# The sum over keys as one instruction, the residual through PSUM, and low halves on GpSimd or VectorE: a four-layer attention and MLP kernel

## The chip, the cores and the metric

The kernel runs on one core of a Trainium2 chip. The core has TensorE (PE, matmuls into the accumulator memory PSUM; its weight loads are PEld), VectorE (DVE), ScalarE (ACT), GpSimd (POOL) and the queue engine SyncE (SP), which issues nearly all DMAs here. Each engine works through its own instructions in order and waits on semaphores of the others. The metric is the device time of one execution in microseconds (us), the median of several runs. A profile is taken in a run of its own.

## What is computed

x has 2048 rows of 640. Four layers follow each other, two of attention (the same weights both times) and two of an MLP:

```python
x = x + _A_ref(_layernorm(x), A_wqkv, A_wo)     # 32 heads of 20; each row looks at 8 keys,
x = x + _B_ref(_layernorm(x), B_w1, B_b1, ...)  # at distance 0, 2, 4, ... 14 behind it
x = x + _A_ref(_layernorm(x), A_wqkv, A_wo)     # MLP: layernorm, 640 -> 1536, gelu, 1536 -> 640
x = x + _B_ref(_layernorm(x), B_w1, B_b1, ...)
...
logits = jnp.einsum("bhsd,bhswd->bhsw", q, kg) * scale
attn = _softmax(logits, axis=-1)
o = jnp.einsum("bhsw,bhswd->bhsd", attn, vg)
```

## The kernel before, in words

**Units.** The distance of two between keys splits the rows into even and odd ones, and each parity into two halves: four units of 512 rows. A unit lies on 128 partitions with four rows each (M = 4, index t). With two attention layers there are eight units of attention, n = 0 to 7; n // 4 is the layer. Each unit has four groups of eight heads, 32 groups in all, G = 4 n + g.

**Precision.** A matmul on 16-bit operands takes every 32-bit operand as a high half and a low half (low = value - high), and adds three products: high x high, high x low, low x high (PASS). So every tensor that goes into a matmul needs an instruction for its high half (ScalarE) and one for its low half. The low halves that matter here: `yl`, of the layer-normed rows (line 617, 640 wide, VectorE); `ol`, of the attention output (line 779, 640 wide, GpSimd for the first three groups of a unit and VectorE for the fourth); `hlo`, of the MLP's hidden values (line 859, 512 wide, or 256 wide for the first unit, VectorE). Weights are kept times 64 (WS).

**One unit.** `layernorm` makes y and its halves and has the DMA transpose them. `qkv` multiplies (line 647), ScalarE copies the result (line 664), and it goes out to DRAM (`spill`), from which `fetch` brings q, k and v back, each partition with the rows of its neighbours that its windows need. `attention(G)` does the rest on VectorE, for two of the four rows at a time (a = 0, 1): multiply q with eight windows of k (line 731, 2560 elements), sum over the 20 elements of a head (line 735, a reduce from 2560 to 128), the softmax on 256 elements (lines 740 to 750, with the exponential on ScalarE; lines 743 and 748 reduce over the eight keys, which lie apart in memory), multiply with eight windows of v (line 757, 2560), and sum over the eight keys by halves: 1280, 640 and 320 elements (lines 765 and 769). `project(n)` transposes the output by DMA, multiplies it with wo in eight products of 15 matmuls (line 803, two column halves of 320 for each t), and line 809 on VectorE adds the result to x. Then `layernorm(..., True)` and `mlp`: line 848 multiplies into a PSUM bank, ScalarE applies gelu (line 854) and takes the high half (line 857), VectorE the low half (line 859), and line 869 multiplies into accumulators. Line 624 on GpSimd adds the bias b2 to x ahead of that. The last two units' MLP is done jointly by `joint` and `pair` with fewer products (lines 907 to 1233); its weights are loaded (line 961) into the buffers `pr`, once the last attention is done with them.

**Order.** Nothing is scheduled by the compiler. Every instruction is entered in a `Plan` with its engine, an estimated duration, a priority, what it needs and gives, and the buffers it uses. `Plan.run` then simulates the core: at each step it takes the engine that can start first and, on it, the ready instruction with the lowest priority number; the order found in this way is the order of the instructions on every engine and queue. Durations are formulas: `v_cost(n)` = 0.067 + n/960 us for VectorE (line 282), plus 0.19 for the reduces of lines 743 and 748, and `a_cost` for ScalarE (line 286). The chip follows the order; it does not follow the times.

**GpSimd beside VectorE.** The plan marks VectorE instructions that read two tensors from SBUF (`PAIRS`, line 66, by the name of what they give) and GpSimd instructions that do so (`pair=True`). For a marked GpSimd instruction the plan looks for a time outside the stretches of marked VectorE instructions (lines 197 to 203), and a marked VectorE instruction is planned after a marked GpSimd instruction that runs longer than 1 us (line 192). Such a GpSimd instruction also gets a dependency on the VectorE instruction planned to end before it (`behind`, lines 269 and 1285). `ol` on GpSimd waits besides for the first multiply of the next group (line 782), and line 624 for certain later groups (line 623), so that both fall beside the reduce of line 735; they are booked at ASIDE = 1.7 us.

**Buffers that matter.** `ps`: three PSUM banks, shared by qkv, the projection and the MLP's first product; `w`: five, for y, its halves and the attention output; `pr`: two, for the products of attention; `h32` and `hh`: two and three, for the hidden values.

Of the kernel before, what the change touches and what calls it, by code (L numbers as in the profile page):

```python
# [12 lines left out]
OP = mybir.AluOpType  # L13
# [52 lines left out]
PAIRS = ("qk", "pv", "ad", "o", "sub", "at", "hlo", "yl", "xb", "ol", "wq", "lo", "lm")  # L66

TURN = 2.7

# [4 lines left out]
class Plan:  # L74
# [35 lines left out]
    def add(self, eng, dur, prio, emit, need=(), give=(), use=(), table=None, move=None, lazy=False, wait=None,  # L110
            pair=False):
        o = dict(eng=eng, dur=dur, prio=prio, emit=emit, need=need, give=give, use=use, table=table,
                 move=move, lazy=lazy, n=len(self.ops), pair=pair,
                 wait=self.PATIENCE * (eng == "dve" and prio < -200) if wait is None else wait)
        self.ops.append(o)
        for u in use:
            if u not in self.users and u[0] in self.ORDERED and u not in self.line.setdefault(u[0], []):
                self.line[u[0]].append(u)
            self.users[u] = self.users.get(u, 0) + 1

    def run(self):
# [3 lines left out]
        left = {}  # L125
        for o in self.ops:
            left[o["n"]] = len(set(o["need"]))
            for k in set(o["need"]):
                waiting.setdefault(k, []).append(o)
            if not left[o["n"]]:  # L130
                ready.setdefault(o["eng"], []).append(o)
# [10 lines left out]
        def done(o, end, lag):  # L142
            for u in o["use"]:
                self.users[u] -= 1
                self.last[u] = max(self.last.get(u, 0.0), end + lag * (u[0] != "pr" or o["eng"] != "dve"))
                if not self.users[u]:
                    self.free[u[0]].append((self.last[u], self.slot[u]))
            for k in o["give"]:
                when[k] = (o["eng"], end, bool(o["move"]))
                for w in waiting.pop(k, ()):  # L150
                    left[w["n"]] -= 1
                    if not left[w["n"]]:
                        ready.setdefault(w["eng"], []).append(w)
# [32 lines left out]
        def start(o):  # L186
            t = clock[o["eng"]]
# [3 lines left out]
            if o["pair"] and o["eng"] == "dve":  # L191
                t = max(t, port)
            for k in o["need"]:
                e, w, moved = when[k]
                w = w + (self.LAG["sp"] + self.SPARE[o["eng"]] if moved else self.LAG[e] if e != o["eng"] else 0.06 * (e != "pe"))
                t = max(t, w)
            if o["pair"] and o["eng"] == "pool":
                for i, (a, b) in enumerate(reversed(shut)):
                    if t >= b:
                        break  # L200
                    if a <= t:
                        t = b + 0.1 * (i == 0)
                        break
            new = {}
            for u in o["use"]:
                if u in self.slot:
                    t = max(t, self.since[u])
                else:
                    fs = self.free[u[0]]
                    if u[0] in self.ORDERED and self.line[u[0]][self.turn.get(u[0], 0)] != u:  # L210
                        return None
                    i = new.get(u[0], 0)
                    if i >= len(fs):
                        return None
                    t = max(t, sorted(fs)[i][0])
                    new[u[0]] = i + 1
            return t

        total = len(self.ops)
        while len(order) < total:  # L220
            best = None
            for e, ops in ready.items():
                pick = None
                for o in ops:
                    t = start(o)
# [5 lines left out]
                if pick and (best is None or (pick[1], pick[0]) < (best[1], best[0])):  # L231
                    best = pick
            then = event()
            if best is None and then == math.inf:
# [4 lines left out]
            _, t, o = best  # L239
            e = o["eng"]  # L240
            ready[e].remove(o)
            d = o["dur"]
# [24 lines left out]
            elif e == "pool" and o["pair"] and d > 1:  # L267
# [22 lines left out]
def sliding_dilated_then_mlp_kernel(  # L290
# [128 lines left out]
    def pool(dur, prio, emit, need=(), give=(), use=(), pair=False):  # L419
        plan.add("pool", dur, prio, emit, need, give, use, pair=pair)  # L420
# [120 lines left out]
    def layernorm(n, prio, yk, twice):  # L541
# [56 lines left out]
        for t in range(m):  # L598
# [13 lines left out]
            if n == 0 and not twice:  # L612
# [4 lines left out]
            dve(D, first(t), lambda key=key, parts=parts: nc.vector.tensor_sub(parts()[:, 1], tile_of(*key), parts()[:, 0]),  # L617
                need=[("yh", name, t)], give=[("yl", name, t)], use=[key, nk, hk])
# [3 lines left out]
            if twice and n != PAIR[0]:  # L622
                G, a = NG * n + ((6, 1), (7, 1), (8, 0), (8, 1))[t][0], (1, 1, 0, 1)[t]
                pool(ASIDE, -200 + n, lambda t=t: nc.gpsimd.tensor_add(x[u][:, t], x[u][:, t], b2),  # L624
                     need=[("y", name, t), ("qk", G, a), "b2"], give=[("xb", n, t)], pair=True)
# [73 lines left out]
    def attention(G):  # L699
# [52 lines left out]
        for a in range(NE):  # L752
# [10 lines left out]
            last = ("pv", G, a)  # L763
            for w in (4, 2):
                dve(EH * w * GC, G - 0.9, lambda vk=vk, w=w: nc.vector.tensor_add(  # L765
                    tile_of(*vk)[:, :, 0:w], tile_of(*vk)[:, :, 0:w], tile_of(*vk)[:, :, w:2 * w]),
                    need=[last], give=[("ad", G, a, w)], use=[vk])
                last = ("ad", G, a, w)
            dve(EH * GC, G - 0.9, lambda vk=vk, t0=t0: nc.vector.tensor_add(
                ot()[:, t0:t0 + EH], tile_of(*vk)[:, :, 0], tile_of(*vk)[:, :, 1]),  # L770
                need=[last], give=[("o", G, a)], use=[vk, ok])
# [9 lines left out]
        if g < NG - 1:  # L781
            pool(ASIDE, -300 + G, lambda: lo(nc.gpsimd), need=[("oh", G), ("qk", G + 1, 0)], give=[("ol", G)], use=[ok, hk],
                 pair=True)
        else:
            dve(m * GC, -300 + G, lambda: lo(nc.vector), need=[("oh", G)], give=[("ol", G)], use=[ok, hk])

    def project(n):
# [3 lines left out]
        for t in range(m):  # L791
            dma_transpose(-600 + n, lambda t=t: nc.sync.dma_start_transpose(
                transposed(yk)[:, :, t * P:(t + 1) * P], tile_of(*hk)[:, t].rearrange("p a b -> p (a b)")),
                need=[("ol", n * NG + g) for g in range(NG)], give=[("oT", n, t)], use=[hk, yk])
        for t in range(m):
            for c in range(2):
                pk = ("ps", ("wo", n, t, c))

                def product(t=t, c=c, pk=pk):
                    i = 0  # L800
                    for k in range(KD):
                        for a, b in PASS:
                            nc.tensor.matmul(tile_of(*pk)[:, :D // 2], transposed(yk)[:, a * KD + k, t * P:(t + 1) * P],  # L803
                                             wo[:, b, k, c * D // 2:(c + 1) * D // 2], start=i == 0, stop=i == 3 * KD - 1)
                            i += 1

                def residual(t=t, c=c, pk=pk):
                    xs = x[u][:, t, c * D // 2:(c + 1) * D // 2]
                    nc.vector.scalar_tensor_tensor(xs, tile_of(*pk)[:, :D // 2], 1.0 / WS, xs, op0=OP.mult, op1=OP.add)  # L809

                mm(3 * KD * D // 2, 15, -600 + n, product, need=[("oT", n, t), *[("lo", ("o", k)) for k in range(KD)]],
                   give=[("wop", n, t, c)], use=[pk, yk])
                dve(D // 2, -700 + n, residual, need=[("wop", n, t, c)], give=[("xh", n, t, c)], use=[pk])
# [4 lines left out]
    def mlp(at, b, t0, t1):  # L818
# [17 lines left out]
        for e in range(NF):  # L836
# [7 lines left out]
            def inner(ck=ck, pk=pk):  # L844
# [14 lines left out]
            dve(nt, -1000, lambda h32=h32, hk=hk: nc.vector.tensor_sub(  # L859
                tile_of(*hk)[:, 1, :nt], tile_of(*h32)[:, :nt], tile_of(*hk)[:, 0, :nt]),  # L860
                need=[("hhi", j)], give=[("hlo", j)], use=[h32, hk])
# [454 lines left out]
```

## Time and profile before

| | us |
|---|---|
| median of 3 runs | 1147.57 |
| lowest, highest | 1146.56, 1148.22 |
| the profiled execution | 1150.09 |
| its span, first to last instruction | 1148.3 |

The page of the profile gives busy times of each engine, the chain of work that ended last, and groups of instructions. A group's row reads: line, engine, operation, output<-input with shapes, xcount | busy us, mean ns of one | idle time of the engine ahead of it and what ended it. In the timeline the columns are start, duration, engine, line, operation. L12 is line 12 of the kernel before. In the view of waits a row is: engine and line <- what ended its wait: total us, times, longest.

### The profile page before, as it was taken

The numbers are of one execution on the slowest core, as the hardware profiler recorded it, in microseconds if no ns is written. First come the engines' busy times: TensorE is split into PE (matmuls) and PEld (weight loads), VectorE is DVE, ScalarE is ACT, GpSimd is POOL, SyncE is SP. The second block draws the span as 40 slices with busy tenths as digits, with TensorE's granted clock in tenths as the row PEclk, the third lists the DMA queues.
The fourth block names the chain that finished last, engine by engine and source line by source line (L and its number), as shares of the span: only waits on it lengthen the run. The fifth ranks groups of instructions, "written<-read, shape, count | busy, mean of one in ns | idle before, by whom it ended". The sixth has DMA issues, their size and how long they took to land.

```text
span 1148.3 us, 17448 instructions
## 1 busy us (share of the span) xinstructions
PE 1138.7 (99%) x6834; PEld 629.9 (55%) x6834; DVE 1070.0 (93%) x1099; ACT 551.5 (48%) x989; POOL 111.9 (10%) x94
## 2 busy tenths in 40 slices
PE   9999999999999999999999999999999999999998
PEld 6444446577664455545555554556456555644476
DVE  7899999999999999999999999999999998599982
ACT  6385435536355336732637362375333533477630
POOL 1010001011012102210112011101110000000000
PEclk9999999999999999999999999999999999999999
DMA  9999999888875587577475956567756754796201
GB/s 302 297 305 266 299 342 280 279 265 258 242 202 188 171 230 165 184 201 220 131 225 159 216 157 211 180 180 176 214 181 174 200 194 134 192 249 180 62 25 69
DMA packets 239791, 235.47 MB, mean 205 GB/s; under 512 B 139020, under 2 KB 195164, under 8 KB 239708
## 3 DMA queue, kind: packets, MB, share of 16 engines
q1 hardware_dynamic: 239708, 234.36, 69.6%
q8 instruction: 53, 0.87, 0.3%
q14 instruction: 30, 0.25, 0.1%
HBM read 157.55 MB, written 44.78 MB: 176 GB/s over the span
## 4 chain that ended last, share of the span: by engine, by line
PE 91%; DVE 4%; DMA 2%; issue 1%; ACT 1%; SPq 0%; POOL 0%; POOLq 0%; ACTq 0%
PE ps L647 34%; PE acc L869 19%; PE ps L848 18%; PE ps L803 11%; PE acc L1041 3%; PE ps L1076 3%; PE ps L1041 2%; DVE pr L973 1%; DVE pr L731 1%; PE acc L1237 1%; DMA c<-mw 1%; DMA yT<-ohl 1%; PE acc L1076 1%; DVE yT L988 0%; DMA yT<-w 0%
## 5 line engine op out<-in xcount | busy, mean ns | idle before, releaser
L647 PE MATMUL ps<-wq,yT 128*128 128x480 f16 (+1 forms) x1950 | 391.2, 363 | 0.5 <-DMA yT<-w 0.3
L647 PEld LDWEIGHTS <-yT 128*128 128x128 f16 x1950 | 189.2, 98 | 199.3 <-DMA yT<-w 0.7
L869 PE MATMUL acc<-c,act 128*128 128x512 f16 (+1 forms) x1728 | 248.3, 299 | 0.1
L848 PE MATMUL ps<-yT,c 128*128 128x512 f16 (+1 forms) x1260 | 246.5, 349 | 1.0 <-DMA c<-mw 1.0
L869 PEld LDWEIGHTS <-act 128*128 128x128 f16 x1728 | 136.0, 98 | 106.1 <-issue 0.4
L731 DVE TENSOR_TENSOR pr<-qk 128x2560 f32<-128x2560 f32 x64 | 180.6, 2823 | 4.6 <-DMA qk<-spill 4.4
L735 DVE TENSOR_REDUCE sm<-pr 128x128 f32<-128x2560 f32 x64 | 179.7, 2810 | 0.1
L757 DVE TENSOR_TENSOR pr<-sm,v 128x2560 f32<-128x2560 f32 x64 | 179.5, 2820 | 0.3
L848 PEld LDWEIGHTS <-c 128*128 128x128 f16 x1260 | 120.2, 98 | 107.8 <-DMA c<-mw 1.7
L664 ACT ACTIVATE ev<-ps 128x480 f32<-128x480 f32 x128 | 72.5, 567 | 181.1 <-PE ps L647 167.9
L765 DVE TENSOR_TENSOR pr<-pr 128x1280 f32<-128x1280 f32 (+1 forms) x128 | 144.8, 1153 | 0.1
L803 PE MATMUL ps<-wo,yT 128*128 128x320 f16 x960 | 131.9, 299 | 0.7 <-DMA yT<-ohl 0.7
L854 ACT ACTIVATE act<-ps,b 128x512 f32<-128x512 f32 (+1 forms) x84 | 52.4, 624 | 164.8 <-PE ps L848 164.4
L803 PEld LDWEIGHTS <-yT 128*128 128x128 f16 x960 | 93.8, 98 | 38.7 <-DMA yT<-ohl 1.1
L569 ACT ACTIVATE junk<-xf 128x640 f16<-128x640 f32 x57 | 41.9, 735 | 80.4 <-DVE xf L809 68.3
L779 POOL TENSOR_TENSOR ohl<-w,ohl 128x640 f16<-128x640 f32 x24 | 34.2, 1427 | 365.1 <-DVE pr L731 215.5
L586 POOL TENSOR_TENSOR ln<-ln,half 128x2 f32<-128x2 f32 (+1 forms) x31 | 34.9, 1126 | 340.8 <-ACT ln L583 340.6
L859 DVE TENSOR_TENSOR act<-act 128x512 f16<-128x512 f32 (+1 forms) x84 | 51.2, 610 | 9.5 <-ACT act L857 9.2
L624 POOL TENSOR_TENSOR xf<-xf,b 128x640 f32<-128x640 f32 x24 | 37.9, 1578 | 165.2 <-DVE act L859 61.9
L609 ACT ACTIVATE w<-xf,ln 128x640 f32<-128x640 f32 x53 | 47.1, 909 | 3.1 <-DVE w L617 3.1
L857 ACT ACTIVATE act<-act 128x512 f16<-128x512 f32 (+1 forms) x84 | 47.5, 566 | 2.0
L573 ACT ACTIVATE junk<-xf,ln 128x640 f16<-128x640 f32 x57 | 46.9, 822 | 0.8
(194 smaller groups left out, 955.9 us busy)
## 6 DMA issues: line engine op xcount, KB each, us to landing
c<-mw SPq DMA_DIRECT2D x174, 320.0 KB, 3.7
spill<-ev SPq DMA_DIRECT2D x64, 480.0 KB, 4.2
qk<-spill SPq DMA_DIRECT2D x32, 880.0 KB, 5.8
v<-spill SPq DMA_DIRECT2D x32, 880.0 KB, 5.3
qk<-spill SPq DMA_DIRECT2D x32, 320.0 KB, 3.2
act<-in_B_w_dram SPq DMA_DIRECT2D x24, 320.0 KB, 4.9
mw<-c SPq DMA_DIRECT2D x24, 320.0 KB, 4.9
pr<-in_B_w_dram SPq DMA_DIRECT2D x24, 320.0 KB, 3.8
```

Source lines behind the costliest of these rows:

```text
L647: nc.tensor.matmul(ps, transposed(yk)[:, a * KD + k, t * P:(t + 1) * P], wq[:, b, k, g, i0:i1], start=first and j == 0, stop=last and j == ...
L664: act(3 * GC, -400 + n, lambda i=i, pk=pk, ek=ek: nc.scalar.activation(tile_of(*ek)[:, :, i], tile_of(*pk)[:, :3 * GC].rearrange("p (a c) ...
L731: nc.vector.tensor_mul(tile_of(*pk), w[:, HALO + m + t0:HALO + m + t0 + EH, None, :].to_broadcast([P, EH, W, GC]), windows(w, t0, [GC, W], ...
L735: dve(E, G - 0.7, lambda pk=pk, t0=t0: nc.vector.tensor_reduce(lg(t0, t0 + EH).rearrange("p t w h -> p (t w h)"), tile_of(*pk).rearrange(" ...
L757: nc.vector.tensor_mul(tile_of(*vk).rearrange("p t w (h d) -> p t (w h) d", d=DH), lg(t0, t0 + EH).rearrange("p t w h -> p t (w h)")[:, :, ...
L765: dve(EH * w * GC, G - 0.9, lambda vk=vk, w=w: nc.vector.tensor_add(tile_of(*vk)[:, :, 0:w], tile_of(*vk)[:, :, 0:w], tile_of(*vk)[:, :, w ...
L803: nc.tensor.matmul(tile_of(*pk)[:, :D // 2], transposed(yk)[:, a * KD + k, t * P:(t + 1) * P], wo[:, b, k, c * D // 2:(c + 1) * D // 2], s ...
L848: nc.tensor.matmul(tile_of(*pk)[:, :nt], tile_of(*ck)[:, a, k * P:(k + 1) * P], transposed(yk)[:, c * KD + k, t0 * P:t1 * P], start=i == 0 ...
L854: act(nt, -430, lambda pk=pk, h32=h32, e=e: nc.scalar.activation(tile_of(*h32)[:, :nt], tile_of(*pk)[:, :nt], AF.Gelu_apprx_tanh, bias=b1[ ...
L859: dve(nt, -1000, lambda h32=h32, hk=hk: nc.vector.tensor_sub(tile_of(*hk)[:, 1, :nt], tile_of(*h32)[:, :nt], tile_of(*hk)[:, 0, :nt]), nee ...
L869: nc.tensor.matmul(accs[k][:, c0:c0 + n], tile_of(*hk)[:, a, (i - t0) * P:(i - t0 + 1) * P], tile_of(*wk)[:, c, w0:w0 + n], start=first, s ...
L1041: nc.tensor.matmul(tile_of(*to(i))[:, :HALF], hl()[:, a, i * P:(i + 1) * P], row(c), start=start and (a, c) == PASS[0], stop=(a, c) == PAS ...
```

## The change

It has four parts.

1. **Sum over keys.** The three adds of lines 763 to 771 become one reduce over the eight keys, with the keys innermost in the access, from 2560 to 320 elements. The plan books it at `v_cost(2560)` + PVR, with PVR = 0.05. The names `ad` and `o` leave PAIRS.
2. **Residual.** In all units but n = 1, ScalarE first writes 64 x into the PSUM bank (`xw`); the projection's matmuls all accumulate onto it (none has the start flag), and ScalarE copies bank / 64 back to x. Unit 1 keeps the VectorE instruction; the first unit's MLP, whose products are 256 wide, uses the same banks around that time.
3. **Low halves.** `yl`, `ol` and `hlo` are entered by a new function `either`: the plan may place them on VectorE or, for 512 and 640 elements, on GpSimd at 1.25 and 1.45 us (POOLED). The 256-wide `hlo` have no GpSimd price. `defer` holds the VectorE choice back by a time after its inputs are there: 2 us for `hlo` (units after the first), 12 or 3 us for `yl` (ahead of attention or of the MLP, units after the first), 20 us for `ol` of the first three groups.
4. **Where GpSimd may run.** An instruction with a GpSimd alternative, or with `fit=True` (line 624's addition of b2, now without its wait for a certain group and booked at 1.65), starts on GpSimd only after the start of a VectorE instruction that is not in PAIRS, and only if it ends by 0.1 us after that one. If nothing else can be placed, one is forced.

The parameters and fields (`alt`, `defer`, `fit`) that carry this through `Plan.add` and `Plan.run`, cut to the core:

```diff
-PAIRS = ("qk", "pv", "ad", "o", "sub", "at", "hlo", "yl", "xb", "ol", "wq", "lo", "lm")
+PAIRS = ("qk", "pv", "sub", "at", "hlo", "yl", "xb", "ol", "wq", "lo", "lm")
...
+PVR = 0.05
+HDEF, YDEF, ODEF = 2.0, (12.0, 3.0), 20.0
+POOLED = {512: 1.25, 640: 1.45}
...
+        def enter(o):
+            ready.setdefault(o["eng"], []).append(o)
+            if o["alt"]:
+                ready.setdefault("pool", []).append(o)
...
-        def start(o):
-            t = clock[o["eng"]]
+        def start(o, eng, forced=False):
+            t = clock[eng]
+            fit = eng == "pool" and (o["alt"] or o["fit"])
...
+            t = max(t, at + (o["defer"] if eng == "dve" else 0.0))
+            if o["pair"] and eng == "pool" and not fit:
...
+            if fit and not forced:
+                d = o["alt"] or o["dur"]
+                if not past or past[-1]["pair"]:
+                    return None
+                a, b = past[-1]["at"] + 0.08, past[-1]["at"] + past[-1]["dur"]
+                t = max(t, a)
+                if t + d > b + 0.1:
+                    return None
             return t
...
+    def either(n, prio, emit, need=(), give=(), use=(), defer=0.0):
+        plan.add("dve", v_cost(n), prio, emit, need, give, use, pair=give[0][0] in PAIRS, alt=POOLED.get(n), defer=defer)
+        o = plan.ops[-1]
+        o["emit"] = lambda: emit(nc.gpsimd if o["eng"] == "pool" else nc.vector)
...
-            dve(D, first(t), lambda key=key, parts=parts: nc.vector.tensor_sub(parts()[:, 1], tile_of(*key), parts()[:, 0]),
-                need=[("yh", name, t)], give=[("yl", name, t)], use=[key, nk, hk])
+            either(D, first(t), lambda by, key=key, parts=parts: by.tensor_sub(parts()[:, 1], tile_of(*key), parts()[:, 0]),
+                need=[("yh", name, t)], give=[("yl", name, t)], use=[key, nk, hk], defer=YDEF[twice] * (n > 0))
...
-                G, a = NG * n + ((6, 1), (7, 1), (8, 0), (8, 1))[t][0], (1, 1, 0, 1)[t]
-                pool(ASIDE, -200 + n, lambda t=t: nc.gpsimd.tensor_add(x[u][:, t], x[u][:, t], b2),
-                     need=[("y", name, t), ("qk", G, a), "b2"], give=[("xb", n, t)], pair=True)
+                pool(1.65, -200 + n, lambda t=t: nc.gpsimd.tensor_add(x[u][:, t], x[u][:, t], b2),
+                     need=[("y", name, t), "b2"], give=[("xb", n, t)], fit=True)
...
-            last = ("pv", G, a)
-            for w in (4, 2):
-                dve(EH * w * GC, G - 0.9, lambda vk=vk, w=w: nc.vector.tensor_add(
-                    tile_of(*vk)[:, :, 0:w], tile_of(*vk)[:, :, 0:w], tile_of(*vk)[:, :, w:2 * w]),
-                    need=[last], give=[("ad", G, a, w)], use=[vk])
-                last = ("ad", G, a, w)
-            dve(EH * GC, G - 0.9, lambda vk=vk, t0=t0: nc.vector.tensor_add(
-                ot()[:, t0:t0 + EH], tile_of(*vk)[:, :, 0], tile_of(*vk)[:, :, 1]),
-                need=[last], give=[("o", G, a)], use=[vk, ok])
+            dve(E, G - 0.9, lambda vk=vk, t0=t0: nc.vector.tensor_reduce(
+                ot()[:, t0:t0 + EH], tile_of(*vk).rearrange("p t w c -> p t c w"), axis=AX.X, op=OP.add),
+                need=[("pv", G, a)], give=[("o", G, a)], use=[vk, ok], more=PVR)
...
+        either(m * GC, -300 + G, lo, need=[("oh", G)], give=[("ol", G)], use=[ok, hk], defer=ODEF * (g < NG - 1))
...
+        filled = n != 1
...
-                                             wo[:, b, k, c * D // 2:(c + 1) * D // 2], start=i == 0, stop=i == 3 * KD - 1)
+                                             wo[:, b, k, c * D // 2:(c + 1) * D // 2], start=not filled and i == 0,
+                                             stop=i == 3 * KD - 1, skip_group_check=True)
...
+                if filled:
+                    act(D // 2, -600 + n, lambda part=part, pk=pk: nc.scalar.activation(tile_of(*pk)[:, :D // 2], part(), AF.Copy, scale=WS),
+                        need=[("oT", n, t), ("x", la, u, t), *[("xr", la, u, t)] * la, ("r", ("a", n), t)], give=[("xw", n, t, c)], use=[pk])
...
+                if filled:
+                    act(D // 2, -700 + n, lambda part=part, pk=pk: nc.scalar.activation(part(), tile_of(*pk)[:, :D // 2], AF.Copy, scale=1.0 / WS),
+                        need=[("wop", n, t, c), ("y", ("a", n), t)], give=[("xh", n, t, c)], use=[pk])
+                else:
+                    dve(D // 2, -700 + n, residual, need=[("wop", n, t, c)], give=[("xh", n, t, c)], use=[pk])
...
-            dve(nt, -1000, lambda h32=h32, hk=hk: nc.vector.tensor_sub(
+            either(nt, -1000, lambda by, h32=h32, hk=hk: by.tensor_sub(
                 tile_of(*hk)[:, 1, :nt], tile_of(*h32)[:, :nt], tile_of(*hk)[:, 0, :nt]),
-                need=[("hhi", j)], give=[("hlo", j)], use=[h32, hk])
+                need=[("hhi", j)], give=[("hlo", j)], use=[h32, hk], defer=HDEF * (b > 0))
```

More of the change, by code (lines that the diff above doesn't have):

```diff
@@ L130, in run @@
             if not left[o["n"]]:
[L131 removed]
+                enter(o)
         clock = {e: 0.0 for e in self.LAG}
@@ L224, in run @@
                 for o in ops:
-                    t = start(o)
+                    t = start(o, e)
                     if t is None:
@@ L266, in run @@
                 before = kind
-            elif e == "pool" and o["pair"] and d > 1:
+            elif e == "pool" and (o["pair"] or o["fit"]) and d > 1:
                 port = t + d
```

48 lines of the change are left out of this document (26 added, 22 removed).

## The prediction

> **What bounds the kernel now.** I read the page first: busy times, then the chain that ended last.
>
> ```profile
> span 1148.3 us, 17448 instructions
> PE 1138.7 (99%) x6834; PEld 629.9 (55%) x6834; DVE 1070.0 (93%) x1099; ACT 551.5 (48%) x989; POOL 111.9 (10%) x94
> PE 91%; DVE 4%; DMA 2%; issue 1%; ACT 1%; SPq 0%; POOL 0%; POOLq 0%; ACTq 0%
> ```
>
> TensorE (PE) is busy for all but 9.6 us, and it is 91% of the chain. VectorE (DVE) is second with 93%, yet little waits for it. The change removes no matmul, so what it can win is only idle time of TensorE. The view of waits lists that time by what ended it, and the last matmul shows the tail:
>
> ```profile
> PE acc L1041 <- DMA pr<-in_B_w_dram: 1.4, 1, 1.4
> PE acc L1237 <- POOL ident L446: 1.4, 1, 1.4
> PE ps L848 <- DMA c<-mw: 1.0, 1, 1.0
> PE ps L803 <- DMA yT<-ohl: 0.7, 1, 0.7
> PE acc L1041 <- ACT act L1048: 0.3, 1, 0.3
> PE ps L1076 <- ACT xf L1145: 0.3, 1, 0.3
> PE ps L1076 <- DVE wq L1150: 0.3, 1, 0.3
> PE ps L647 <- DMA yT<-w: 0.3, 1, 0.3
> ...
> 1144.62 0.30 PE L1041 MATMUL acc<-w,act 128*128 128x320 f16 x1
> ```
>
> The last matmul ends at 1144.92, so 3.4 us of the idle time lie behind it; 1.4 us lie ahead of the first warm-up matmul (the row of L1237). Neither is touched. What is left in the middle is 9.6 - 3.4 - 1.4 = 4.8 us: **no outcome can gain more than 4.8 us, 0.4%**. The loss has no such lid. The third view is busy time by stage: units and attention (20 to 960), the last projection, the paired MLP (columns: PE, PEld, DVE, ACT, POOL):
>
> ```profile
> 20.00:960.00 940.00, 937.89 (x5542) 508.20 (x5540) 915.42 (x832) 447.70 (x821) 106.81 (x80) 1.00 0.74 219
> 960.00:1002.00 42.00, 42.00 (x287) 25.33 (x286) 27.82 (x43) 17.03 (x30) 1.10 (x2) 1.00 0.66 168
> 1002.00:1148.30 146.30, 140.43 (x833) 81.13 (x831) 114.93 (x197) 75.15 (x117) 0.76 (x1) 1.00 0.42 115
> ```
>
> In the first stage VectorE idles 940 - 915.4 = 24.6 us of 940. It is close behind TensorE there: VectorE work that grows by more than those 24.6 us becomes the bound. The granted clock is 1.00 throughout and enters no term.
>
> **The change part by part: the sum over keys.** Three adds of 1280, 640 and 320 elements become one reduce over 2560, 64 times. Durations overlap the next instruction by 0.08, so I take start to start in VectorE's timeline; the GpSimd row behind it belongs to the same moment:
>
> ```profile
> 324.66 1.49 DVE L765 TENSOR_TENSOR pr<-pr 128x1280 f32<-128x1280 f32 x1
> 326.06 0.82 DVE L617 TENSOR_TENSOR w<-w,w 128x640 f16<-128x640 f32 x1
> 326.80 0.82 DVE L765 TENSOR_TENSOR pr<-pr 128x640 f32<-128x640 f32 x1
> 327.53 0.42 DVE L740 TENSOR_TENSOR sm<-sm,mask 128x256 f32<-128x256 f32 x1
> 327.87 0.49 DVE L769 TENSOR_TENSOR w<-pr 128x320 f32<-128x320 f32 x1
> 328.27 0.61 DVE L743 TENSOR_REDUCE sm<-sm 128x32 f32<-128x256 f32 x1
> 328.79 2.82 DVE L731 TENSOR_TENSOR pr<-qk 128x2560 f32<-128x2560 f32 x1
> 331.52 0.43 DVE L744 TENSOR_TENSOR sm<-sm 128x256 f32<-128x256 f32 x1
> 331.86 2.82 DVE L735 TENSOR_REDUCE sm<-pr 128x128 f32<-128x2560 f32 x1
> 334.59 0.82 DVE L617 TENSOR_TENSOR w<-w,w 128x640 f16<-128x640 f32 x1
> ...
> 332.17 1.40 POOL L779 TENSOR_TENSOR ohl<-w,ohl 128x640 f16<-128x640 f32 x1 [8.02 <-DVE sm L744]
> ```
>
> The adds cost 1.40 + 0.73 + 0.40 = 2.53 us. The trace has no reduce that is both long and strided. Low bound: L735, same tile, same operation, 2560 elements read in order, 2.73 us. High bound: L743 sums eight values that lie apart, as the new line does; it takes 0.52 where L744 on as many elements takes 0.34. If those 0.18 us grow with the elements (ten times as many), the reduce takes 2.73 + 1.8 = 4.53 us; if they are a fixed price, 2.91. L735 speaks against a fixed price for reduces as such, not against one for this access. I take the low end, 2.73 to 2.8. Size, tile and output are nearest to L735; and the plan in the code books this line at 2.73 + 0.05. That is a claim, but where the trace can check the plan's prices they hold within 0.02: 2.73 for 2560 elements, 0.33 + 0.19 = 0.52 for L743, 0.33 for L744. So the exchange costs +0.2 us, 64 x 0.2 = +13 us of VectorE (high bound 64 x 2.0 = +128).
>
> The Trainium skill, Vector Engine (DVE) Microarchitecture Reference, section 5.2, speaks against this part: a stream that hops at every element ran at 1.73 ns per element against 1.05. For 2560 elements that would be 4.4 us, close to the high bound; L743 agrees (0.18 us over 256 elements is 0.70 ns each). The same section reports a one-source operation whose reads alternate between two far regions at the full rate; no run here shows that.
>
> **Residual.** In seven of eight units (not n = 1) the L809 instruction leaves VectorE; ScalarE writes x times 64 into the bank ahead of the product, and copies it back after.
>
> ```profile
> L809 DVE SCALAR_TENSOR_TENSOR xf<-ps,xf 128x320 f32<-128x320 f32 x64 | 30.1, 487 | 11.7 <-PE ps L803 11.2
> L803 PE MATMUL ps<-wo,yT 128*128 128x320 f16 x960 | 131.9, 299 | 0.7 <-DMA yT<-ohl 0.7
> L664 ACT ACTIVATE ev<-ps x128: 545/570/602, 15.1 to 843.3; 128x480 f32<-128x480 f32 x128
> L1141 ACT ACTIVATE ps<-ev x3: 584/586/601, 1043.1 to 1059.7; 128x512 f32<-128x512 f32 x3
> ```
>
> VectorE loses 56 x (0.487 - 0.08) = -23 us. ScalarE gains 112 instructions; 480 elements take 0.57 and 512 take 0.59, so 320 take about 0.45 (estimate from those two rows): +50 us on an engine that is 48% busy, hidden while it stays ahead. The cover: a product takes 131.9/64 = 2.06 us, three banks turn in 6.2 us, and one bank now needs 0.45 + 2.06 + 0.45 = 2.96 us, which leaves 3.2 us for signals and for what stands ahead in ScalarE's queue (layer norms, gelus). The new wait: a fill stands in ScalarE's queue until the transposed attention output has landed; behind it are gelus and layer norms, on which MLP matmuls wait. Where TensorE already waits for that landing (the 0.7 us above) the fill adds its 0.45 and a hand-over of 0.15, 0.6 us in all. Low bound 0, high bound 0.6 in each of seven projections, 4.2; I take one, 0.6.
>
> **Low halves.** hlo (512 wide), yl and ol may now run on GpSimd, but only where the plan finds room beside a VectorE instruction that reads one SBUF tensor; until then VectorE holds its own copy back by 2 to 20 us.
>
> ```profile
> L859 DVE TENSOR_TENSOR act<-act 128x512 f16<-128x512 f32 x60 | 41.2, 687 | 9.4 <-ACT act L857 9.2
> L617 DVE TENSOR_TENSOR w<-w,w 128x640 f16<-128x640 f32 x56 | 44.8, 819 | 1.4 <-ACT w L615 1.2
> L779 POOL TENSOR_TENSOR ohl<-w,ohl 128x640 f16<-128x640 f32 x24 | 34.2, 1427 | 365.1 <-DVE pr L731 215.5
> L624 POOL TENSOR_TENSOR xf<-xf,b 128x640 f32<-128x640 f32 x24 | 37.9, 1578 | 165.2 <-DVE act L859 61.9
> ...
> 386.32 1.54 POOL L779 TENSOR_TENSOR ohl<-w,ohl 128x640 f16<-128x640 f32 x1 [12.81 <-DVE sm L743]
> 386.52 4.02 DVE L731 TENSOR_TENSOR pr<-qk 128x2560 f32<-128x2560 f32 x1
> ```
>
> The place matters: at 332.17 GpSimd ran beside a reduce and the reduce kept its 2.82 us; at 386.32 it ran beside a multiply of two tensors, which took 4.02 instead of 2.82, +1.2 us. With the new sums there are 128 long reduces. Demand: 60 hlo, two to a reduce if one takes about 1.25 us (between 1.12, four fifths of the 1.40 of 640 elements, and 1.40 itself), 30 places; 56 yl, 32 ol and 24 additions of b2, one each: 142 places for 128. So not all move. Movable from VectorE: 60 x 0.60 + 56 x 0.74 = 77 us; I take three quarters, -58 (bounds half and all, -38 and -77). What is late next: a hlo held back 2 us delays TensorE's low pass, a yl delays a transpose on SP's queue; both have the high-half matmuls and other units' products as cover, and if the cover is gone each costs its delay.
>
> **The sum.** VectorE: +13 - 23 - 58 = -68 us, almost all in the first stage, 7% of it. That shortens the end of attention:
>
> ```profile
> 974.80 0.89 DVE L769 TENSOR_TENSOR w<-pr 128x320 f32<-128x320 f32 x2
> 975.71 2.09 SPq L961 DMA_DIRECT2D pr<-in_B_w_dram  x4
> ```
>
> The last QKV result leaves ScalarE at 843.3 (the L664 row) and the last sum ends at 975.7, where the weights of the paired MLP begin to load. Those 132 us, 7% shorter, bring these loads some 9 us forward, past the 1.4 us wait for them; the three 0.3 us waits of the pair and the two for transposes (0.7, 0.3) are late VectorE work too. That is 1.4 + 0.9 + 1.0 = 3.3 us; the wait for MLP weights (1.0) stays. With the new 0.6: 3.3 - 0.6 = **2.7 us less**. The profiled execution took 1150.09 with a span of 1148.3; the median of the runs is 1147.57. The span should become 1145.6 and the median 1147.57 - 2.7 = **1144.9 us**.
>
> **The rivals.** (1) The gaps are hidden anyway: they come from loads and transposes in a fixed order, VectorE's relief turns into VectorE idling, and the new 0.6 eats what little closes: 1147 us. For it: TensorE at 99%, and five of eight waits name a DMA or GpSimd. This is also the case in which the change does what it says and nothing follows.
>
> (2) The strided sum takes 4.53 us. VectorE then grows by 128 - 23 - 58 = 47 us; 24.6 us of idle absorb part and 23 us come out at the end, since attention's end at 975.7 moves by as much and projection and pair still follow: 1147.6 + 23 = 1171 us (1152 if all 77 us move, 1191 if half). It decides from 2.53 + (23 + 58 + 24.6)/64 = 4.18 us per sum. For it: L743. Against: L735. The hopping stream of the Trainium skill, named above, is this rival; by it the time would be about the same.
>
> (3) The waits: fills exposed in all seven projections (4.2 us) and some low halves late for TensorE, say one in ten of the 60 hlo by its 1 us beyond cover (6 us), because the order on each queue is fixed from planned prices: about 10 us, of which 2.7 are won back: 1155 us. For it: GpSimd's queue is in order, and one misplaced instruction costs 1.2 us. Against: 68 us of released VectorE time cover 56 such collisions.
>
> **How the numbers follow.** About 0.2%, 2.3 us, is what a measurement can tell from no change: 1145.3 and 1149.9 are the borders. Forecast 0.45, rival (1) 0.14, rival (2) 0.23, rival (3) 0.18. So faster 0.45, same 0.14, slower 0.41. The forecast alone has the range 1142.7 (all 4.8 us) to 1145.3. The range over the cases is 1142.7 to 1170: it holds the forecast, (1), (3) and half of (2), and leaves out about 0.13.
>
> **What would show it right or wrong.** Right: the new sum's group near 2.8 us; VectorE busy near 1002 us; L809 eight times; ScalarE near 600 us; GpSimd's groups of 512 and 640 near 1.25 and 1.43, with multiplies of 2560 still at 2.82; fewer PE waits behind 1002. Wrong: a sum at 4.2 us or more and PE waits on transposed attention (yT<-ohl), which is rival (2); PE waits on ScalarE's fills or on GpSimd's act tiles, rival (3); the same eight waits, rival (1).

## The result and the profile after

The changed kernel takes 1251.13 us (median of 4 runs, 1250.13 to 1252.58) against 1147.89 us for the kernel before: 103 us slower, ratio 1.0906 with a 95% interval of 1.0893 to 1.0919. The forecast was 1144.9 us, the range ended at 1170.

The page of the changed kernel, the same three lines as before the change:

```profile
span 1249.2 us, 17385 instructions
PE 1169.7 (94%) x6834; PEld 638.8 (51%) x6834; DVE 1144.8 (92%) x880; ACT 597.3 (48%) x1107; POOL 159.6 (13%) x129
DVE 32%; PE 15%; issue 8%; ACT 1%; DMA 1%; SPq 0%; DVEq 0%; ACTq 0%
```

The chain has changed hands: VectorE, 4% before, is now its largest share, with TensorE at 15% after 91% (the shares add up to 57% of the span, since the chain is followed back only to 534 us; their ratio is what to read). TensorE's idle time went from 9.6 us to 1249.2 - 1169.7 = 79.5 us, and the same 6834 matmuls take 31.0 us more. These two, 69.9 and 31.0, are the whole difference of the spans, 100.9 us.

The groups of VectorE, then ScalarE and GpSimd, that the change touches (row: xcount | busy us, mean ns of one | idle ahead):

```profile
L796 DVE TENSOR_REDUCE w<-pr 128x320 f32<-128x2560 f32 x64 | 293.0, 4597 | 0.1
L764 DVE TENSOR_TENSOR pr<-qk 128x2560 f32<-128x2560 f32 x64 | 179.6, 2813 | 23.2 <-DMA qk<-spill 23.2
L768 DVE TENSOR_REDUCE sm<-pr 128x128 f32<-128x2560 f32 x64 | 179.5, 2807 | 0.1
L651 DVE TENSOR_TENSOR w<-w,w 128x640 f16<-128x640 f32 x38 | 30.9, 820 | 0.0
L893 DVE TENSOR_TENSOR act<-act 128x512 f16<-128x512 f32 x44 | 30.3, 689 | 1.5 <-ACT act L891 1.5
...
L844 ACT ACTIVATE xf<-ps 128x320 f32<-128x320 f32 x56 | 23.8, 426 | 21.7 <-PE ps L827 21.3
L839 ACT ACTIVATE ps<-xf 128x320 f32<-128x320 f32 x56 | 23.6, 433 | 0.4
...
L651 POOL TENSOR_TENSOR w<-w,w 128x640 f16<-128x640 f32 x18 | 25.3, 1403 | 92.6 <-ACT w L649 30.8 <-issue 19.0 <-DVE act L893 7.4
L893 POOL TENSOR_TENSOR act<-act 128x512 f16<-128x512 f32 x16 | 18.5, 1158 | 118.2 <-ACT act L891 43.9 <-DVE pr L790 23.5 <-DVE w L796 18.4
```

The new sum (L796) takes 4.60 us; the plan books 2.78. The reduce of the logits (L768), as many elements read in order, takes 2.81. Only 18 of 56 `yl` and 16 of 60 `hlo` went to GpSimd. VectorE's timeline gives the price from start to start:

```profile
329.64 4.62 DVE L796 TENSOR_REDUCE w<-pr 128x320 f32<-128x2560 f32 x1
334.17 0.89 DVE L836 SCALAR_TENSOR_TENSOR xf<-ps,xf 128x320 f32<-128x320 f32 x2
```

That is 4.53 us, 2.0 more than the three adds. Busy times up to the end of the last sum and after it (columns: PE, PEld, DVE, ACT, POOL, clock, DMA), first before, then after:

```profile
20.00:975.70 955.70, 953.59 (x5634) 516.15 (x5632) 929.26 (x846) 453.32 (x828) 107.22 (x80) 1.00 0.73 217
975.70:1148.30 172.60, 166.73 (x1026) 98.50 (x1024) 128.91 (x225) 86.56 (x139) 1.44 (x2) 1.00 0.49 130
```

```profile
20.00:1064.50 1044.50, 979.14 (x5608) 522.38 (x5607) 1005.78 (x633) 490.09 (x925) 154.82 (x115) 0.97 0.67 197
1064.50:1249.20 184.70, 172.17 (x1050) 101.46 (x1047) 126.66 (x220) 95.11 (x159) 1.60 (x2) 0.97 0.48 128
```

Attention ends 88.8 us later: VectorE has 76.5 us more work by then and idles 12.3 us more (38.7 instead of 26.4). What follows takes 12.1 us longer than before. TensorE's waits in the changed kernel:

```profile
PE acc L903 <- DVE xf L938: 18.9, 8, 6.4
PE ps L680 <- DMA yT<-w: 11.5, 3, 4.8
PE ps L827 <- DMA yT<-ohl: 9.9, 2, 8.6
PE ps L827 <- ACT ps L839: 9.7, 4, 5.6
PE ps L680 <- ACT ev L697: 8.5, 3, 4.0
PE acc L903 <- DVE act L893: 6.9, 5, 3.0
PE acc L903 <- ACT act L891: 6.8, 2, 6.6
...
PE acc L903 <- POOL act L893: 0.2, 1, 0.2
```

Most names in this list are not VectorE, and GpSimd's low halves stand for 0.2 us. A reader who stops here would blame the fills (L839) or the transposes. The chain, as far back as it goes, runs mostly over VectorE. It does not reach the waits ahead of 534 us, so the experiments have to decide.

### The profile page after: what moved, and what is told of

The parts are those of the page before. It is cut to its first block, busy times and chain, and to the rows that moved or that the text cites. A ratio compares the mean times of both kernels' runs of the same rounds, so it can differ in the third digit from the quotient of the medians.

```text
span 1249.2 us, 17385 instructions
## 1 busy us (share of the span) xinstructions
PE 1169.7 (94%) x6834; PEld 638.8 (51%) x6834; DVE 1144.8 (92%) x880; ACT 597.3 (48%) x1107; POOL 159.6 (13%) x129
## 4 chain that ended last, share of the span: by engine, by line
DVE 32%; PE 15%; issue 8%; ACT 1%; DMA 1%; SPq 0%; DVEq 0%; ACTq 0%
DVE w L796 9%; DVE pr L764 6%; DVE pr L790 6%; DVE sm L768 5%; PE ps L1110 4%; PE acc L1075 4%; PE ps L827 2%; PE ps L1075 2%; PE acc L903 1%; PE ps L680 1%; DVE w L651 1%; DVE act L893 1%; PE acc L1110 1%; PE ps L882 1%; DVE xf L938 1%
## 5 line engine op out<-in xcount | busy, mean ns | idle before, releaser
L680 PE MATMUL ps<-wq,yT 128*128 128x480 f16 (+1 forms) x1950 | 401.6, 369 | 21.6 <-DMA yT<-w 11.5
L680 PEld LDWEIGHTS <-yT 128*128 128x128 f16 x1950 | 191.8, 99 | 228.9 <-issue 24.0
L796 DVE TENSOR_REDUCE w<-pr 128x320 f32<-128x2560 f32 x64 | 293.0, 4597 | 0.1
L903 PE MATMUL acc<-c,act 128*128 128x512 f16 (+1 forms) x1728 | 261.6, 306 | 33.0 <-DVE xf L938 18.9
L882 PE MATMUL ps<-yT,c 128*128 128x512 f16 (+1 forms) x1260 | 250.1, 352 | 0.0
L903 PEld LDWEIGHTS <-act 128*128 128x128 f16 x1728 | 139.5, 100 | 148.3 <-issue 30.4
L764 DVE TENSOR_TENSOR pr<-qk 128x2560 f32<-128x2560 f32 x64 | 179.6, 2813 | 23.2 <-DMA qk<-spill 23.2
L768 DVE TENSOR_REDUCE sm<-pr 128x128 f32<-128x2560 f32 x64 | 179.5, 2807 | 0.1
L827 PE MATMUL ps<-wo,yT 128*128 128x320 f16 x960 | 138.5, 307 | 19.6 <-DMA yT<-ohl 9.9
L827 PEld LDWEIGHTS <-yT 128*128 128x128 f16 x960 | 95.8, 100 | 61.6 <-DMA yT<-ohl 12.6
L803 ACT ACTIVATE ohl<-w 128x640 f16<-128x640 f32 x32 | 23.5, 735 | 174.5 <-DVE w L796 174.4
L620 POOL TENSOR_TENSOR ln<-ln,half 128x2 f32<-128x2 f32 (+1 forms) x31 | 39.0, 1260 | 248.3 <-ACT ln L617 231.9
L649 ACT ACTIVATE w<-w 128x640 f16<-128x640 f32 x56 | 40.7, 729 | 16.3 <-DMA yT<-w 9.6
```

Source lines behind the costliest of these rows:

```text
L680: nc.tensor.matmul(ps, transposed(yk)[:, a * KD + k, t * P:(t + 1) * P], wq[:, b, k, g, i0:i1], start=first and j == 0, stop=last and j == ...
L764: nc.vector.tensor_mul(tile_of(*pk), w[:, HALO + m + t0:HALO + m + t0 + EH, None, :].to_broadcast([P, EH, W, GC]), windows(w, t0, [GC, W], ...
L768: dve(E, G - 0.7, lambda pk=pk, t0=t0: nc.vector.tensor_reduce(lg(t0, t0 + EH).rearrange("p t w h -> p (t w h)"), tile_of(*pk).rearrange(" ...
L796: dve(E, G - 0.9, lambda vk=vk, t0=t0: nc.vector.tensor_reduce(ot()[:, t0:t0 + EH], tile_of(*vk).rearrange("p t w c -> p t c w"), axis=AX. ...
L882: nc.tensor.matmul(tile_of(*pk)[:, :nt], tile_of(*ck)[:, a, k * P:(k + 1) * P], transposed(yk)[:, c * KD + k, t0 * P:t1 * P], start=i == 0 ...
L903: nc.tensor.matmul(accs[k][:, c0:c0 + n], tile_of(*hk)[:, a, (i - t0) * P:(i - t0 + 1) * P], tile_of(*wk)[:, c, w0:w0 + n], start=first, s ...
```

## The experiments

Three theories had to be told apart. A: the hopping access of the sum (each element read lies 160 words on from the last), 1.8 us each time, is the cause. B: the waits that fills and moved low halves brought. C: an order planned from a wrong price.

### The sum in order, and the three adds back

`adjacent`: the same instruction, as many elements and outputs, the plan untouched, but it adds eight adjacent elements, which is not the attention's sum.

```diff
-                ot()[:, t0:t0 + EH], tile_of(*vk).rearrange("p t w c -> p t c w"), axis=AX.X, op=OP.add),
+                ot()[:, t0:t0 + EH], tile_of(*vk).rearrange("p t w c -> p t (w c)").rearrange("p t (c w) -> p t c w", w=W), axis=AX.X, op=OP.add),
```

> The changed kernel with one edit: the sum over keys reads 2560 elements in order and adds eight adjacent ones, so this kernel computes another sum than the attention's; instruction, count, output and the plan's order stay. Theory A (the access that hops at every element costs 1.8 us a sum, and this alone made the 103 us): the sum takes 2.8 us, the time is 1143 to 1152 us. Theory A' (sums of only eight terms cost, whatever their access): the sum stays at 4.6 us, the time at 1251. Theory B (the waits that the fills on ScalarE and the low halves on GpSimd brought): the sum takes 2.8 us but the time stays above 1200.

Measured 1152.53 us (1151.36 to 1153.20) against 1146.90, ratio 1.0049 (1.0034 to 1.0064). Its group, and TensorE's waits:

```profile
L796 DVE TENSOR_REDUCE w<-pr 128x320 f32<-128x2560 f32 x64 | 178.9, 2814 | 1.4 <-DMA yT<-w 1.3
```

```profile
PE acc L903 <- DMA c<-mw: 5.5, 1, 5.5
PE acc L1271 <- POOL ident L480: 1.3, 1, 1.3
PE ps L882 <- DMA c<-mw: 1.0, 1, 1.0
PE ps L680 <- DMA yT<-w: 0.9, 1, 0.9
PE ps L1110 <- ACT wq L1182: 0.5, 1, 0.5
```

With order, counts, fills and moved low halves all in place, reading in order takes away 98.6 of the 104 us; the 2.81 us also exclude that sums of only eight terms are slow as such. Theory A holds for size, though the time is 0.5 us above its range; B is left with 5.6 us. The last sum now ends 8 us before that of the kernel before, and the pair's waits behind 1002 us fall from 2.3 to 0.5 us. Against that stands one new wait of 5.5 us, for the weights of the first MLP.

`adds`: the changed kernel with the three adds and their names in PAIRS again.

```diff
-            dve(E, G - 0.9, lambda vk=vk, t0=t0: nc.vector.tensor_reduce(
...
+            last = ("pv", G, a)
+            for w in (4, 2):
+                dve(EH * w * GC, G - 0.9, lambda vk=vk, w=w: nc.vector.tensor_add(
```

> The changed kernel with the three adds back in place of the one sum (and their names back in PAIRS, so GpSimd may run only beside the 64 reduces of the logits). Theory A: 1143 to 1152 us, VectorE busy near 1025 us. Theory B: above 1200 us, with TensorE waiting for fills and low halves as before.

Measured 1155.55 us (1155.07 to 1156.40), ratio 1.0078 (1.0062 to 1.0093): theory A, though 3.5 us above its range; VectorE is busy 1034.8 us, 10 us more than expected.

```profile
PE acc L909 <- DVE act L899: 5.9, 2, 3.4
PE ps L833 <- ACT ps L845: 1.2, 1, 1.2
```

The two waits for `hlo`, 5.9 us together, fall between 227 and 244 us, again at the first MLP.

### The true price in the plan

`priced`: one number.

```diff
-PVR = 0.05
+PVR = 1.8
```

> The changed kernel with PVR = 1.8: the plan books the sum at 4.53 us, which it takes. Nothing else changes but the order that follows from it. Theory A (the work itself): VectorE has some 1100 us of work up to the end of attention, so the time stays above 1200 us, 10 to 40 us below 1251. Theory C (the order planned from a wrong price): most of the 103 us come back, the time is below 1190 us.

Measured 1212.93 us (1212.69 to 1215.71), ratio 1.0583 (1.0567 to 1.0598). 38 us come back, at the upper end of what A allowed, well short of C (the 1100 us of VectorE work that A's expectation named were too many, it is 997 from 20 us on). Busy times up to the last sum's end and after, and the two largest waits:

```profile
20.00:1039.00 1019.00, 968.47 (x5709) 522.97 (x5707) 997.03 (x618) 494.72 (x929) 176.81 (x138) 0.98 0.71 206
1039.00:1211.30 172.30, 157.28 (x948) 93.11 (x948) 122.08 (x212) 91.28 (x154) 1.38 (x2) 0.97 0.44 114
```

```profile
PE ps L827 <- DMA yT<-ohl: 35.6, 1, 35.6
PE ps L882 <- DMA yT<-w: 22.7, 2, 16.0
```

Against the changed kernel, attention ends 25.5 us earlier. VectorE has 8.8 us less work by then, as the plan, which now sees a longer sum, puts 29 `yl` and 27 `hlo` on GpSimd instead of 18 and 16, and it idles 16.7 us less; what follows is 12.4 us shorter. So the order is not all that changed, the placing did too.

Against the kernel before, VectorE has 67.8 us more work up to the last sum's end (997.0 - 929.3), idles 4.4 us less (22.0 instead of 26.4), and the rest takes as long as before (172.3 us against 172.6). Work and idle time add up to the span in any run; what these figures show is that idle time and rest are back where they were, so that the growth is VectorE's work. TensorE waits in three large pieces, and its busy time is only 5.5 us above that before. So of the 103 us, about 65 stay as work with this plan, and 38 come from an order and a placing made for a sum of 2.78 us. Whether another order would hide more of the 65 was not tried.

### The sum alone

`sum_only`: the kernel before with the new sum, booked as in the change.

```diff
-            last = ("pv", G, a)
...
+            dve(E, G - 0.9, lambda vk=vk, t0=t0: nc.vector.tensor_reduce(
...
+                need=[("pv", G, a)], give=[("o", G, a)], use=[vk, ok], more=0.05)
```

> The kernel before with the one sum in place of the three adds, booked at 2.73 + 0.05 as in the change; residual and low halves as before. Theory A: 64 x 2.0 = 128 us more on VectorE against 25 us of idle time, nothing taken off it, so 1245 to 1275 us, at or above the changed kernel. Theory B: below 1200 us, as neither fills nor moved low halves are there.

Measured 1267.11 us (1266.31 to 1268.03), ratio 1.1048 (1.1030 to 1.1067): theory A. The other parts of the change win back 16 us of the sum's 120; with them VectorE is busy 1144.8 us instead of 1194.5.

### What makes the access dear

`pairs`: sums over four keys and two adjacent columns, so the same hops of 160 words, but two words after each (another sum than the attention's).

```diff
-                ot()[:, t0:t0 + EH], tile_of(*vk).rearrange("p t w c -> p t c w"), axis=AX.X, op=OP.add),
+                ot()[:, t0:t0 + EH].rearrange("p t c -> p (t c)").rearrange("p (q c) -> p q c", q=2 * EH), tile_of(*vk).rearrange("p t (s w) (c b) -> p (t s) c w b", s=2, b=2), axis=AX.XY, op=OP.add),
```

> The changed kernel with the sum over four keys and two adjacent columns instead of eight keys (another sum than the attention's): 2560 elements, 320 sums of eight, the same hop of 160 words, but in runs of two adjacent words. If each lone word after a hop costs, and a run of two rides free (the rule of the skill's page): sum 2.8 us and the time of the sum in order, about 1152. If each hop costs 0.70 ns: 1280 hops, 3.7 us, about 1195 us. If only sums over spread keys of any kind cost: 4.6 us, 1251.

One execution, 1152.69 us.

```profile
L796 DVE TENSOR_REDUCE w<-pr 128x320 f32<-128x2560 f32 x64 | 178.8, 2813 | 1.4 <-DMA yT<-w 1.2
```

The same 2.81 us as in order: 1280 hops of 640 bytes are free when two words follow each, and 2560 lone words cost 1.79 us.

`moved`: the attention's own sum, with the multiply by v writing key by key (its writes hop 8 words), and the sum reading in order.

```diff
-                    tile_of(*vk).rearrange("p t w (h d) -> p t (w h) d", d=DH),
+                    tile_of(*vk).rearrange("p t w c -> p t (w c)").rearrange("p t (h d w) -> p t w h d", d=DH, w=W),
```

> The attention's own sum again, with the hop moved: the multiply with v writes its products key by key into adjacent words (each write hops 8 words), and the sum reads them in order. If the hop costs on the write side as on the read side: the sum takes 2.8 us, the multiply 4.5 us instead of 2.8, and the time is that of the changed kernel, 1240 to 1260 us. If writes hop free: multiply 2.8, sum 2.8, 1150 to 1155 us, and the change would be had without its price.

One execution, 1254.30 us.

```profile
L790 DVE TENSOR_TENSOR pr<-sm,v 128x2560 f32<-128x2560 f32 x64 | 305.0, 4808 | 0.4
L796 DVE TENSOR_REDUCE w<-pr 128x320 f32<-128x2560 f32 x64 | 178.7, 2812 | 0.1
```

The hop went from the sum to the multiply and cost 0.2 us more there; the time is that of the changed kernel.

### The 5.6 us that the rest of the change costs

The 5.6 us are those of `adjacent`. With the adds back, GpSimd has 64 long reduces to run beside instead of 128, and the loss is 8.7 us (`adds`), so the runs below, which have the adds, need not lose in the same way. `resid_only` is the kernel before with part 2 of the change alone; `halves_only` is `adds` with the residual on VectorE, so parts 3 and 4 alone.

```diff
-        filled = n != 1
+        filled = False
```

> The kernel before with the residual alone changed: ScalarE fills the bank with 64 x and copies it back, in seven of eight units. It asks where the 5.6 us come from that the kernel with the sum in order still lost, 5.5 of them in one wait for the first MLP's weights near 226 us. Theory D (ScalarE's 112 instructions: they stand ahead of weight splits and gelus, or TensorE waits for the fills): 1150 to 1154 us. Theory E (GpSimd and the held-back low halves reorder VectorE's splits of these weights): 1144 to 1148 us here, and the loss in the run with the low halves alone.

> The changed kernel with the three adds back and the residual on VectorE: what is left of the change is low halves and b2 on GpSimd or VectorE, only beside the reduces of the logits. Theory D: 1146 to 1149 us. Theory E: 1152 to 1157 us, with TensorE waiting near 220 to 245 us.

`resid_only`: 1149.18 us (12 runs, 1147.39 to 1156.10) against 1147.04, ratio 1.0027 (1.0009 to 1.0045); the profiled execution took 1147.88. The median lies between the two expectations. Five of the twelve executions took 1151 to 1156 us, and the profiled one is not among them, so what those five waited for is not seen. In the profiled one no TensorE wait is for a fill:

```profile
PE ps L1087 <- ACT xf L1156: 1.6, 1, 1.6
PE acc L880 <- DVE xf L915: 1.3, 1, 1.3
PE ps L647 <- DMA yT<-w: 0.9, 1, 0.9
```

`halves_only`: 1163.33 us (1162.38 to 1163.95), ratio 1.0135 (1.0119 to 1.0151), above even theory E.

```profile
PE acc L909 <- ACT act L897: 5.1, 1, 5.1
PE ps L833 <- ACT act L894: 2.9, 2, 2.3
PE ps L833 <- DVE xf L842: 2.7, 1, 2.7
```

The larger loss sits with parts 3 and 4: 16.3 us alone, 8.7 with the residual on ScalarE beside them. Two more runs asked for the place, both on top of `adds`:

```diff
-HDEF, YDEF, ODEF = 2.0, (12.0, 3.0), 20.0
+HDEF, YDEF, ODEF = 0.0, (0.0, 0.0), 0.0
```

> The changed kernel with the three adds back and without hold-back (HDEF = YDEF = ODEF = 0): VectorE takes a low half as soon as it is its turn, GpSimd only what it can start earlier, which the plan places there 6 times. It asks whether the hold-back makes the 8.7 us that the kernel with the adds back lost. Theory F (hold-back and GpSimd's places delay the first MLP and the layer norms): 1145 to 1150 us. Theory G (VectorE's relief does not matter, but the residual on ScalarE and b2 beside reduces cost): 1153 to 1158 us.

```diff
-HDEF, YDEF, ODEF = 2.0, (12.0, 3.0), 20.0
-POOLED = {512: 1.25, 640: 1.45}
+HDEF, YDEF, ODEF = 0.0, (12.0, 3.0), 20.0
+POOLED = {640: 1.45}
```

> The changed kernel with the three adds back and hlo on VectorE alone, without hold-back; yl and ol as in the change. TensorE's longest waits in the kernel with the adds back ended with hlo (5.9 us in two). If hlo's places cause the loss: 1146 to 1150 us. If it is yl and ol (the layer norms' results and the weight splits that wait behind them): 1153 to 1158 us.

`no_hold` took 1151.48 us (1150.26 to 1152.58), ratio 1.0035 (1.0022 to 1.0047), between its two theories; `hlo_back` 1157.17 (1153.40 to 1157.93), ratio 1.0078 (1.0058 to 1.0098), so moving `hlo` back changes nothing. What is left is `yl`, `ol` and the new places of b2, which no run told apart. Taking the hold-back away, and with it all but 6 of GpSimd's low halves, halves the loss. In both, TensorE's longest wait still falls at the first MLP (3.3 us for its weights in the one, 3.0 us for `hlo` in the other, between 229 and 244 us). In `adds` the chain into the last wait there runs over VectorE, whose attention instructions of 2.7 us each stand ahead of `hlo`. Which of the new places puts them there is not settled. None of these kernels beats the one before.

## Why the prediction was wrong, step by step

**The lid.** No outcome was to gain more than 4.8 us. No kernel here gained anything measurable, also where VectorE lost 36 us of work (`adjacent`, DVE 1033.9 us). The reading that TensorE was the bound of the kernel before was right.

**The price of the sum: the step that failed.** The prediction put it between 2.73 and 4.53 us and took the low end, since "size, tile and output are nearest to L735" and the plan's other prices held. The sum took 4.53 us from start to start in the timeline above, the high bound to the hundredth. The nearest row was the small L743, which shares the access, not the large L735, which shares the size:

```profile
L743 DVE TENSOR_REDUCE sm<-sm 128x32 f32<-128x256 f32 x32 | 19.5, 609 | 0.3
L744 DVE TENSOR_TENSOR sm<-sm 128x256 f32<-128x256 f32 x32 | 13.5, 422 | 0.3
```

The excess per element is 0.70 ns for the new sum ((4597 - 2807) / 2560) and 0.73 for L743 against L744 ((609 - 422) / 256). That the plan's prices matched the trace said nothing about this one, as each matched price belonged to an access which that kernel already ran. The Trainium skill, Vector Engine (DVE) Microarchitecture Reference, section 5.2, was right on both sides: lone words after a hop cost 0.68 ns each (an estimate from its table, 1.73 against 1.05), and runs of two are free. Its one-source stream at full rate, which I set against it, did not carry over: this one-source reduce paid in full.

**The residual.** 56 instructions left VectorE; the row fell from 30.1 to 3.7 us. ScalarE's fill and copy take 0.433 and 0.426 us (estimate 0.45), ScalarE is busy 597 us (forecast near 600). In the profiled execution of `resid_only` TensorE waits for no fill. The 9.7 us of such waits in the changed kernel are gone in `adjacent`, and in `priced` too, where the sum still takes 4.6 us; in `adds` 1.2 us are left. The forecast's hand-over of 0.15 us between fill and product stands in no trace; after one fill of the changed kernel the first matmul started 0.06 us behind its end (198.84 to 198.90).

**The low halves.** The places beside reduces and GpSimd's durations were judged rightly: 1.16 us for 512 elements, 1.40 for 640, and multiplies of 2560 stayed at 2.81. The term was mis-sized: 18 `yl`, 16 `hlo` and one `ol` are 13.3 + 9.6 + 0.7 = 24 us off VectorE, not 58. The plan gives an instruction to whichever engine can start it first, and so the number depends on hold-back and on booked prices: 6 move without hold-back (`no_hold`), 29 `yl` and 27 `hlo` with the sum booked at 4.53 (`priced`). And the cover named for held-back low halves did not hold at the first MLP.

**The sum of it.** With the sum at its booked price (`adjacent`) attention did end 8 us earlier (9 forecast) and the pair's waits did close, 2.3 to 0.5 us. That the 9 us fit is in part luck: they were worked out from 68 us less on VectorE, and it lost 36. The forecast would still have been wrong by 7.6 us: the new wait at the first MLP is no term of it, and rival (3) had named fills and low halves, not weights.

**Rival (2).** It was the mechanism, with the right price and a place on VectorE up to the end of attention, but its 1171 us were 80 too low. Three things were missing, and they add up to the difference of the spans. Its 47 us of added work on VectorE were 76.5, as some 34 us less moved away. Its 24.6 us of idle time to be used up became 12.3 us more idle time; VectorE's largest wait is for `qk<-spill`, 23.2 us against 4.4 before. That this data was late because of matmuls which themselves waited for VectorE, in a fixed order, is argued, not shown; with the right price in the plan (`priced`) these waits are 3.5 us. And what follows attention took 12.1 us longer. Within all this the matmuls themselves became slower (below). The sign named for rival (3), waits on fills, showed too, but these waits are gone once the sum reads in order or is booked at its price.

## What to carry to other kernels

Price an instruction that the trace does not show by the row that shares its access pattern, even if that row is ten times shorter, and scale its excess by elements; here size and operation mattered less. A saving on an engine that is not the bound buys nothing, while a cost on the engine 25 us behind the bound was paid almost in full: 67.8 us of work, 66 us of time in `priced`. Where an order is fixed from planned prices, one wrong price costs twice, here 65 us as work and 38 us as order and placing, so measure the new instruction by itself before planning with it.

## What the runs showed of the hardware

**Hops.** Read by VectorE, a lone 4-byte word after a hop costs 0.70 ns more than a word read in order, for hops of 160 words (L796) nearly as for 8 words (L743, 0.73). Written, 0.78 ns for hops of 8 words ((4808 - 2820) / 2560 in `moved`). Two adjacent words after each hop cost nothing (`pairs`, 2813 ns against 2814 in order).

**Matmuls after a wait.** TensorE's timeline in the changed kernel, around one wait, and a steady stretch behind it:

```profile
670.39 4.45 PE L903 MATMUL acc<-c,act 128*128 128x128 f16 x16 [3.00 <-DVE act L893]
674.64 3.66 PE L882 MATMUL ps<-yT,c 128*128 128x512 f16 x15
...
686.64 3.42 PE L903 MATMUL acc<-c,act 128*128 128x512 f16 x24
689.90 3.40 PE L882 MATMUL ps<-yT,c 128*128 128x512 f16 x15
```

In the steady stretch, 24 matmuls of L903, twelve of 512 columns and twelve of 128, take 3.26 us. The 16 behind the wait are twelve of 512 and four of 128. They should take 2.8 us (an estimate: 3.26 less eight of 128, of which four take 0.23 us just behind the wait). They take 4.25 us to the next group's start, and that group takes 0.26 us longer than the steady one: 1.7 us in all, on top of the wait. The granted clock shows where (columns as above). First the 3.41 us ahead of the slow stretch and the stretch itself, then the sums over all such stretches, first of the changed kernel, then of `priced`:

```profile
668.34:671.75 3.41, 1.36 (x10) 0.78 (x11) 3.41 (x3) 3.02 (x5) 0.00 (x0) 1.00 0.54 211
671.75:675.16 3.41, 3.41 (x10) 1.18 (x9) 3.41 (x2) 0.03 (x1) 0.00 (x0) 0.50 0.00 0
...
sum 71.67, PE 56.41 PEld 27.14 DVE 61.45 ACT 33.98 POOL 4.18; mean PE 4.03 PEld 1.94 DVE 4.39 ACT 2.43 POOL 0.30
sum 58.02, PE 12.20 PEld 5.16 DVE 48.65 ACT 20.21 POOL 8.02; mean PE 4.07 PEld 1.72 DVE 16.22 ACT 6.74 POOL 2.67
```

The clock is 0.50 for 3.41 us, and half of that is the 1.7 us. Between 149 and 1078 us the changed kernel has fourteen such stretches, each 3.41 us or a whole multiple of it. TensorE is busy for 56.4 us of them; half of that, 28.2 us, accounts for most of the 31.0 us by which the busy time of the same matmuls grew. In `priced` there are three stretches of 58.0 us in all against 71.7, but they fall mostly into the long waits: TensorE is busy for only 12.2 us of them, which makes 6.1 us, near the 5.5 us by which its busy time grew. So the mean clock, 0.97 and 0.98, does not tell the loss. The Trainium skill, TensorE: Matmul & The Clock Gate, Part 1, has the array at half clock after an idle window of about 3.4 us. The length of the stretches agrees with that window; the idling does not quite, since the 3.41 us ahead of this stretch still hold 1.36 us of matmuls. Many waits of a few us are therefore dearer, for the matmuls behind them, than one of 35.6 us.
